# Turning blocks by DMA instead of TensorE in a recurrent-memory attention kernel

## The chip, the cores and the metric

The kernel runs on one core of one Trainium2 chip. The metric is the time of one execution on the device in microseconds (us), taken as the median of several runs.

## The reference, cut to what matters

```python
h  = x + A(_layernorm(x))                 # x: 2048 tokens x 512
h2 = h + B(_layernorm(h))                 # B: layernorm, 512 -> 1792, gelu, 1792 -> 512

def A(x):                                 # 64 segments of 32 tokens, one after the other
    mem = mem0                            # 8 rows
    for s in range(64):
        h = concat([mem, x[32*s : 32*s+32]])            # 40 rows
        q, k, v = h @ Wq, h @ Wk, h @ Wv                # 32 heads of 128
        p = softmax(where(mask, q @ k.T * scale, -1e9))
        o = (p @ v) @ Wo
        mem = o[:8]                                     # goes into the next segment
        outs.append(o[8:])
    return concat(outs)
```

The memory rows are a recurrence: segment s+1 cannot start its projections before segment s has its output projection.

## The kernel before

All weights of part A lie in SBUF from the first 50 us on. Phase 1 handles the 64 segments in order; phase 2 is the MLP on four groups of 512 tokens. Four segments of 32 tokens make a *block* of 128 tokens (16 blocks, `bk`; `sg` is the segment within the block, 0 to 3).

The input rows of a block come by DMA into a slot of `xr`. `ln1(tb)` normalises block `tb` (statistics on VectorE, DVE, the root on GpSimd, POOL) into `xn`, and turns it: four 128x128 transposes on TensorE (PE) into PSUM (`quad`, line 619), then two copies into the stationary operands, `hT` (24 token columns of each segment, line 629) and `hB` (the last 8 token columns of each of the four segments, line 628). Their place in `hT` is taken by the 8 memory rows that the segment before leaves there (line 915).

A segment consists of parts, each a short list of PE instruction groups and of the work on other engines behind them:

- `Q0, Q1, K0, K1, V0, V1`: projections by halves of the heads, four groups each (`one_pass`, line 654). A group is four matmuls side by side in column strips (128*32), one for each quarter of the PSUM bank's partitions. Where two groups in a row use the same stationary operand, its load is left out (`keep`, `matmul_kept`, line 427); `BACK` names passes that run over the contraction in reverse to make that possible.
- A copy of the bank to `kqP` (ACT or DVE, lines 668 and 669) and a 32x32 DVE transpose (line 696) give K and Q by head; `ZC` (lines 666 and 722, POOL) collects query columns for the scores.
- `SC0, SC1`: scores of the rows that need the recurrence (line 796) on a prefilled mask (line 779), then the softmax: maximum `nmc` (804), exponential `EC` (808, ACT), `rsc` (811), `PC` (814), `PTC` (815).
- `PV0, PV1`: weighted sums (lines 826, 830), with row strips (32*128), into `quad`; copies to `OT` and `OTB`.
- `SA`: the scores of the other 24 rows (line 855) and their softmax `PA` (870, POOL or DVE), `PTA` (872). `PVA` (line 881, also 32*128) is their weighted sum, one segment later.
- `WO`: the output projection in eight units (line 909), a DVE transpose `TT` (921), and the additions into `hT` of the next segment and into `opT` (915).
- `F0, F1, FB`: projections of the `hB` rows of the next block (K, Q, V) and the output projection `wo_B` of the block before, which fill PE while the recurrence goes through other engines.
- `TR`: `ln1(bk + 3)` in `sg` 1, and `nat(bk - 2)` in `sg` 0.

`nat(bk)` turns a finished block of `opT` back to rows with four PE transposes into `quad` (line 946). `nat_add` adds them to `xr` on DVE (955), takes statistics for the second layernorm and stores the rows to `h_mid` (962). Both PSUM results of `TR` are read after PV1 of the same segment:

```python
elif name == "TR":
    if sg == 0 and bk > 1:
        after_pv1(nat(bk - 2))
    if s in (1, 2):
        after_pv1(ln1(s + 1))
    elif sg == 1 and bk + 3 < NTB:
        after_pv1(ln1(bk + 3))
```

The order on PE is written out in `ORDER`, one list for each `sg`: `("Q0", 0, 3)` is groups 0 to 2 of that part. `BANKS` gives each part a PSUM bank. The order on all other engines comes from a planner (`Sched.schedule`): every operation has an expected duration (`dur`), a time for handing over (`HOP`, 2.0 us after a DMA), a rank, and a bonus by kind (`BONUS`); it is put into the first gap of its engine that holds it. Where an operation has a choice of engine (`either`), the earliest end decides, with `LEAN` us added for DVE. A DMA is expected to take 0.07 us and a 390th of a us for each KB, plus the 2.0. Operations without a choice wait in the order so planned: an engine never passes over an instruction that waits. All DMAs are issued by one queue, SP's.

PE's instruction stream is cut into basic blocks ("lines") of about 256 instructions by `far` (line 318). Each ends with a conditional branch that is never taken; its target is the line after the next one, and a hint is marked at the start of each line except the first (`mark_branch_hint_location`).

Of the kernel before, what the change touches and what calls it, by code (L numbers as in the profile page):

```python
# [21 lines left out]
LINE_N, LINE_AT, LINE_HINT = 256, 192, 168  # L22
HALVES = ("kqP", "KA", "ZCm", "QA", "VS", "nmc", "EC", "rsc", "PC", "PTC", "OTm", "KB", "QTB", "VSB", "QT")
BONUS = {"EC0": 0.93, "EC1": -5.34, "KA0": 13.28, "KA1": -9.68, "KB0": 21.59, "KB1": 28.09, "OTB": 0.99, "OTm0": 1.34, "OTm1": 17.4,
         "OTx": 13.15, "PA": 5.1, "PC0": 10.61, "PC1": 1.08, "PTA": -17.15, "PTC1": 2.21, "QT0": 2.01, "QT1": 40, "QTB0": 40, "QTB1": -5.37,
         "SA": -0.92, "TT": 17.86, "TTB": 32.47, "VBD": -40, "VS0": 8.39, "VS1": -1.27, "VSB0": 3.04, "VSB1": 40, "ZCb": -29.51,
         "ZCm0": -8.01, "ZCm1": 4.83, "ag": -16.93, "ag2": 3.08, "hB": -4.35, "hTm": 40, "hTx": 40, "hd": 1.51, "hx": -40, "kqP0": -1.06,
         "kqP1": 22.77, "kqP2": -1.2, "kqP3": -8.45, "kqP4": -7.07, "kqP5": -5.84, "nma": 40, "nmc0": -3.19, "nmc1": 0.4, "opA": -6.6,
         "opB": 14.93, "ps": -5.46, "rs": -7.45, "rs2": 11.04, "rsa": 13.98, "rsc1": 1.67, "sma": 8.62, "st": -40, "st2": -14.59,
         "vd": 17.77, "xr": 40}  # L30
LEAN = 0.297
# [4 lines left out]
          (("Q0", 0, 1), ("K0", 0, 2), ("Q0", 1, 2), ("K0", 2, 3), ("Q0", 2, 4), ("K0", 3, 4), ("Q1", 0, 4), ("K1", 0, 4), ("SC0", 0, 1),  # L36
           ("V0", 0, 1), ("TR", 0, 1), ("PVA", 0, 1), ("V0", 1, 4), ("V1", 0, 1), ("SC1", 0, 1), ("F1", 0, 1), ("V1", 1, 2), ("PV0", 0, 1),
           ("V1", 2, 4), ("F0", 0, 2), ("WO", 0, 2), ("PV1", 0, 1), ("WO", 2, 8), ("F1", 1, 2), ("F0", 2, 4), ("F1", 2, 4), ("SA", 0, 1)),
          (("Q0", 0, 3), ("K0", 0, 2), ("Q0", 3, 4), ("K0", 2, 3), ("Q1", 0, 1), ("K0", 3, 4), ("K1", 0, 1), ("Q1", 1, 4), ("K1", 1, 4),
           ("SC0", 0, 1), ("V0", 0, 1), ("PVA", 0, 1), ("V0", 1, 4), ("V1", 0, 2), ("SC1", 0, 1), ("TR", 0, 1), ("PV0", 0, 1),  # L40
           ("F0", 0, 1), ("V1", 2, 4), ("WO", 0, 4), ("PV1", 0, 1), ("F0", 1, 3), ("WO", 4, 8), ("F0", 3, 4), ("F1", 0, 4), ("SA", 0, 1)),
          (("K0", 0, 3), ("Q0", 0, 1), ("K0", 3, 4), ("Q0", 1, 4), ("Q1", 0, 4), ("K1", 0, 4), ("SC0", 0, 1), ("V0", 0, 1), ("PVA", 0, 1),
           ("V0", 1, 2), ("TR", 0, 1), ("V0", 2, 3), ("V1", 0, 1), ("V0", 3, 4), ("V1", 1, 2), ("SC1", 0, 1), ("V1", 2, 4), ("PV0", 0, 1),
           ("F0", 0, 1), ("F1", 0, 2), ("F0", 1, 2), ("WO", 0, 2), ("PV1", 0, 1), ("WO", 2, 8), ("F1", 2, 3), ("F0", 2, 4), ("F1", 3, 4),
           ("SA", 0, 1)),
          (("Q0", 0, 3), ("K0", 0, 2), ("Q0", 3, 4), ("K0", 2, 4), ("Q1", 0, 4), ("K1", 0, 4), ("SC0", 0, 1), ("PVA", 0, 1), ("V0", 0, 2),
           ("FB", 0, 1), ("V0", 2, 4), ("V1", 0, 1), ("SC1", 0, 1), ("V1", 1, 2), ("FB", 1, 2), ("V1", 2, 3), ("PV0", 0, 1), ("V1", 3, 4),
           ("FB", 2, 3), ("TR", 0, 1), ("FB", 3, 4), ("WO", 0, 2), ("PV1", 0, 1), ("WO", 2, 8), ("FB", 4, 7), ("SA", 0, 1), ("FB", 7, 8)),
)
BANKS = (  # L50
    dict(Q0=4, Q1=7, K0=6, K1=5, V0=6, V1=7, SC0=4, SC1=4, F0=6, F1=5, FB=5, SA=7, WO=4),
    dict(Q0=4, Q1=7, K0=6, K1=5, V0=6, V1=7, SC0=4, SC1=4, F0=6, F1=5, FB=5, SA=7, WO=4),
    dict(Q0=4, Q1=7, K0=6, K1=5, V0=6, V1=7, SC0=4, SC1=4, F0=6, F1=5, FB=4, SA=7, WO=4),
    dict(Q0=4, Q1=7, K0=6, K1=5, V0=6, V1=7, SC0=4, SC1=4, F0=6, F1=7, FB=5, SA=7, WO=4),
)
BACK = (("Q1", "K1", "V0", "F1"), ("Q0", "Q1", "K0", "K1", "V0", "F1"), ("K0", "K1", "V0"), ("Q0", "K0", "K1", "V0"))
# [26 lines left out]
class Sched:  # L83
# [234 lines left out]
    def far(self, nc, e, zero):  # L318

        ops = self.streams["pe"]  # L320
        n, lines, cuts = 0, -1, []
        for i, o in enumerate(ops):
            line, at = divmod(n - LINE_AT, LINE_N)
            if line > lines and at >= LINE_HINT:
                assert at < 240
                cuts.append(i)
                lines = line
                n += 2
            n += o.ni + (len(o.waits) >= 2)
        home, mark, k = nc.cur_bb.parent, None, 0  # L330
        for i, o in enumerate(ops):
            if k < len(cuts) and cuts[k] == i:
                if k + 2 < len(cuts):
                    b = e.br_lt(zero, 0, on_true="line%d" % (k + 2), on_false="line%d" % k)
                    if mark is not None:
                        b.branch_hint(mark)
                    nc.switch_bb("line%d" % k, parent=home)
                    mark = e.mark_branch_hint_location()
                else:
                    e.br("line%d" % k)  # L340
                    nc.switch_bb("line%d" % k, parent=home)
                k += 1
            yield o
# [51 lines left out]
ALU = mybir.AluOpType  # L395
AX = mybir.AxisListType

P = 128
# [46 lines left out]
def build_kernel(nc, A_x, A_mem0, A_Wq, A_Wk, A_Wv, A_Wo, B_w1, B_b1, B_w2, B_b2, out):  # L445
# [3 lines left out]
    with st:  # L449
# [10 lines left out]
        hT = sb("hT", [P, RING, DC, SEG])  # L460
        hB = sb("hB", [P, RBLK, DC, SEG])
        xr = sb("xr", [P, XR, D])
# [142 lines left out]
        def ln1(tb):  # L605
# [8 lines left out]
                 reads=[("xr", tb % XR), ("ag", i), ("rs", i)], writes=[("xn", i)], dur=0.405)  # L614
            pb = qbf(128)
# [7 lines left out]
            def ev():  # L623
                src = pb.rearrange("p c (s t) -> p c s t", s=4)
                r0 = 4 * (tb % RBLK)
                dA = hT[:, r0:r0 + 4, :, 0:NA].rearrange("p s c t -> p c s t")
                dB = hB[:, tb % RBLK, :, :].rearrange("p c (s t) -> p c s t", s=4)
                S.either(copy2(dB, src[:, :, :, NA:SEG], 128), reads=QK, writes=[("hB", tb % RBLK)])
                S.either(copy2(dA, src[:, :, :, 0:NA], 384), reads=QK, writes=[("hTx", tb % RBLK)])
            return ev  # L630

        def mem0_T(bank):
            pb = psbf(bank)

            def tr(e):
                for cc in range(DC):
                    ins = e.transpose(pb[:, cc * MEM:(cc + 1) * MEM], m0[0:MEM, cc * P:(cc + 1) * P], ident[0:MEM, 0:MEM])
                return ins
            S.op("pe", tr, reads=["m0", "ident"], writes=[("ps", bank)], dur=0.2, mode=MF)
            S.op("act", lambda e: e.copy(hT[:, 0, :, NA:SEG], pb[:, 0:DC * MEM].rearrange("p (c m) -> p c m", c=DC)),  # L640
                 reads=[("ps", bank)], writes=[("hTm", 0)], dur=t_act(32))
# [36 lines left out]
        def pack_a(s):  # L678
            sl = s % RING
            return ("A", s), (lambda cc: hT[:, sl, cc, :]), [("hTx", (s // 4) % RBLK), ("hTm", sl)]  # L680
# [14 lines left out]
        def pair_T(dst, i, key):  # L695
            S.op("dve", lambda e: e.transpose(dst.bitcast(U32), kqP[:, i, :].bitcast(U32)), reads=[("kqP", i)], writes=[key], dur=0.445)  # L696
# [85 lines left out]
        def sc_mm(s, r, bank):  # L782
# [4 lines left out]
            def f(e):  # L787
                for i in range(4):
# [11 lines left out]
                 writes=[("ps", bank)], dur=0.116, mode=MC, ni=32)  # L800

        def sc_softmax(s, r, bank):
            v = ps[bank][:, 0:128].rearrange("p (a t) -> p a t", a=2)
            S.op("dve", lambda e: e.tensor_reduce(nmc[:, r, :], v, AX.X, ALU.max, negate=True), reads=[("ps", bank)], writes=[("nmc", r)], dur=0.287)  # L804
# [40 lines left out]
        def sa_mm(s, bank):  # L845
# [12 lines left out]
            S.op("pe", f, reads=[("QT", 0), ("QT", 1), ("KA", par, 0), ("KA", par, 1)], writes=[("ps", bank)], dur=0.24, mode=MC, ni=64)  # L858
# [9 lines left out]
            S.op("dve", lambda e: e.tensor_reduce(sma[:], SA[:], AX.X, ALU.add), ["SA"], ["sma"], dur=0.41)  # L868
# [48 lines left out]
        def wo(s, bank, mem=True, xrows=True):  # L917
# [4 lines left out]
            if mem:  # L922
                sl = (s + 1) % RING
                S.op("dve", lambda e: [halves_add(tt, q2, hT[64 * q2:64 * q2 + 64, sl, :, NA:SEG], slice(NA, SEG))(e) for q2 in range(2)][1],
                     reads=[("TT", par)], writes=[("hTm", sl)], dur=0.39)
# [6 lines left out]
        def wo_B(bk, bank):  # L932
# [5 lines left out]
                 reads=["TTB"], writes=[("opB", bk % 2)], dur=0.6)  # L938

        def nat(bk):  # L940
            pb = qbf(192)
            xs = xr[:, bk % XR, :]
# [8 lines left out]
        def nat_add(bk):  # L951
# [3 lines left out]
            S.op("dve", lambda e: e.tensor_tensor(x4, x4, pb, ALU.add), reads=QK + [("xr", bk % XR)], writes=[("xr", bk % XR)], dur=0.41)  # L955
            i = bk % 2
# [32 lines left out]
        hx0, xn0 = xr[:, 2:6, :], view(hT, 4 * DC * SEG, [P, TBS, D])  # L989
# [65 lines left out]
        for s in range(NS):  # L1055
# [29 lines left out]
            def part(name):  # L1085
# [26 lines left out]
                elif name == "TR":  # L1112
                    if sg == 0 and bk > 1:
                        after_pv1(nat(bk - 2))
                    if s in (1, 2):
                        after_pv1(ln1(s + 1))
                    elif sg == 1 and bk + 3 < NTB:
                        after_pv1(ln1(bk + 3))
# [153 lines left out]
```

## Time and profile before

| | |
|---|---|
| median of 8 runs | 861.92 us (859.62 to 865.55) |
| profiled execution, own time | 867.18 us |
| its span, first to last instruction | 865.5 us |
| PE matmuls, busy | 803.8 us, 22,285 instructions |
| DVE, ACT, POOL busy | 544.3, 587.1, 144.0 us |
| granted TensorE clock, mean | 0.984 |
| DMA moved | 40.45 MB, 47 GB/s mean |

The times of the runs spread over 6 us. The profiled execution is one of them in kind, and took 5.3 us more than the median. Times in the profile are those of that execution; busy times of PE include overlap of one matmul with the next, so a single duration (380 ns for a 128x512 matmul) is more than the distance at which they follow each other.

### The profile page before, as it was taken

Reading aid. Unit: us, or ns where it says so; the run is one execution under the profiler, and the core shown is the slowest. Engines: PE = TensorE matmul, PEld = TensorE weight load, DVE = VectorE, ACT = ScalarE, POOL = GpSimd, SP = SyncE. Lnnn points to the kernel's source line nnn. Section 1 sums busy time; section 2 is a strip of 40 time slices with the busy share of each in tenths; the row PEclk is TensorE's granted clock in tenths of the full one; section 3 lists DMA queues with packets and bytes.
Section 4 is the critical chain, followed back from the end, with each engine's and each line's share of the span. In section 5 each row is a group of like instructions: output and inputs, shape, how many; then the busy total and the mean of one; then the engine's idle time right before and its main releaser. Section 6 shows DMA issues by size and latency. Waiting matters only on the chain.

```text
span 865.5 us, 48049 instructions
## 1 busy us (share of the span) xinstructions
PE 803.8 (93%) x22285; PEld 438.1 (51%) x21141; DVE 544.3 (63%) x1683; ACT 587.1 (68%) x1602; POOL 144.0 (17%) x341
## 2 busy tenths in 40 slices
PE   2568899999999999899999999999999998889998
PEld 0134455555555555455555555555555554544443
DVE  2137676778777777677778786767676776532111
ACT  1237677878787878677878787878777776624442
POOL 3012111212121212111111111111111111042200
PEclk9879999999999999999999999999999999999999
DMA  8771001010101010101010101010101110601000
GB/s 337 278 226 40 3 5 28 16 29 16 32 14 34 12 34 10 28 15 29 16 28 17 27 17 28 11 27 11 28 11 29 34 28 9 219 16 48 25 25 25
DMA packets 35303, 40.45 MB, mean 47 GB/s; under 512 B 2452, under 2 KB 31004, under 8 KB 35100
## 3 DMA queue, kind: packets, MB, share of 16 engines
q1 hardware_dynamic: 35100, 37.38, 13.3%
q8 instruction: 172, 2.82, 1.3%
q14 instruction: 31, 0.25, 0.1%
HBM read 28.98 MB, written 8.39 MB: 43 GB/s over the span
## 4 chain that ended last, share of the span: by engine, by line
PE 84%; DVE 7%; DMA 3%; ACT 2%; issue 2%; SPq 1%; POOL 0%; DVEq 0%
PE ps L654 39%; PE ps L909 17%; PE ps L427 6%; PE quad L1169 6%; PE ps L1162 6%; PE quad L826 3%; PE ps L796 2%; PE quad L881 2%; PE ps L855 2%; DMA WQ<-in_A_Wq_dram 1%; DVE opT L937 1%; DMA xr<-in_A_x_dram 1%; ACT EC L808 1%; DVE QT L696 1%; SPq L757 1%
## 5 line engine op out<-in xcount | busy, mean ns | idle before, releaser
L909 PE MATMUL ps<-WO,OT 128*32 128x256 bf16 x4224 | 141.6, 276 | 7.0 <-issue 5.0
L654 PE MATMUL ps<-WV,hT 128*32 128x512 bf16 x1796 | 147.1, 387 | 0.2
L654 PE MATMUL ps<-WQ,hT 128*32 128x512 bf16 x1804 | 133.2, 384 | 3.9 <-DVE hT L915 3.9
L654 PE MATMUL ps<-WK,hT 128*32 128x512 bf16 x1736 | 127.8, 379 | 1.5 <-DVE hT L915 1.1
L909 PEld LDWEIGHTS ps<-WO,OT 128*32 128x32 bf16 x4224 | 102.8, 97 | 38.5 <-ACT OT L668 12.9
L669 ACT ACTIVATE kqP<-ps 128x512 bf16<-128x512 f32 x159 | 95.2, 599 | 30.6 <-PE ps L654 28.4
L668 ACT CAST OT<-quad 128x128 bf16<-128x128 f32 (+1 forms) x177 | 80.9, 457 | 35.6 <-PE quad L830 21.2
L668 ACT CAST kqP<-ps 128x512 bf16<-128x512 f32 x160 | 91.9, 583 | 16.0 <-PE ps L654 13.7
L870 POOL TENSOR_TENSOR PA<-SA,rsa 128x256 bf16<-128x256 f32 x64 | 40.9, 639 | 367.3 <-DVE rsa L869 342.3
L808 ACT ACTIVATE EC<-ps,nmc 128x64 f32<-128x64 f32 x256 | 78.0, 310 | 17.6 <-DVE nmc L804 13.0
L921 DVE STREAM_TRANSPOSE TT<-ps 128x256 f32<-128x256 f32 x66 | 29.7, 450 | 84.0 <-PE ps L909 84.0
L1165 ACT ACTIVATE WQ<-ps,b1t 128x512 bf16<-128x512 f32 x56 | 38.5, 687 | 61.5 <-PE ps L1162 61.0
L654 PEld LDWEIGHTS ps<-WQ,hT 128*32 128x32 bf16 x1804 | 48.7, 97 | 62.0 <-issue 25.2
L668 ACT CAST VS<-ps 128x512 bf16<-128x512 f32 x112 | 65.5, 585 | 20.6 <-PE ps L654 11.3
L654 PEld LDWEIGHTS ps<-WK,hT 128*32 128x32 bf16 x1736 | 47.7, 97 | 54.2 <-issue 16.5
L696 DVE STREAM_TRANSPOSE KALL<-kqP 128x256 uint32<-128x256 uint32 x160 | 64.9, 412 | 11.3 <-ACT kqP L668 11.0
L867 ACT ACTIVATE SA<-SA 128x256 f32<-128x256 f32 x64 | 26.7, 417 | 53.2 <-DVE SA L866 53.2
L696 DVE STREAM_TRANSPOSE QT<-kqP 128x256 uint32<-128x256 uint32 x128 | 55.1, 431 | 4.7 <-ACT kqP L669 4.2
L796 PEld LDWEIGHTS ps<-KALL,ZC 128*32 128x32 bf16 x2048 | 30.9, 96 | 49.7 <-DVE rsc L811 20.4
L1169 PE MATMUL quad<-WK,WQ 128*128 128x512 bf16 x224 | 54.4, 379 | 0.5 <-DVE xr L955 0.5
L654 PEld LDWEIGHTS ps<-WV,hT 128*32 128x32 bf16 x1796 | 40.9, 97 | 24.5 <-issue 13.5
L1213 DVE TENSOR_TENSOR WV<-quad,WV 128x512 bf16<-128x512 f32 x16 | 11.1, 691 | 66.0 <-PE quad L1169 66.0
(116 smaller groups left out, 1371.3 us busy)
## 6 DMA issues: line engine op xcount, KB each, us to landing
WV<-in_A_Wv_dram SPq DMA_DIRECT2D x4, 1024.0 KB, 6.5
WK<-in_A_Wk_dram SPq DMA_DIRECT2D x4, 1024.0 KB, 8.0
v_last<-VSB SPq DMA_DIRECT2D x64, 64.0 KB, 2.1
WQ<-in_A_Wq_dram SPq DMA_DIRECT2D x4, 1024.0 KB, 7.8
VBD<-v_last SPq DMA_DIRECT2D x64, 64.0 KB
WO<-in_A_Wo_dram SPq DMA_DIRECT2D x4, 1024.0 KB, 9.3
WK<-in_B_w_dram SPq DMA_DIRECT2D x2, 1792.0 KB, 13.3
xr<-in_A_x_dram SPq DMA_DIRECT2D x16, 128.0 KB, 2.2
```

The costliest lines, as they stand in the source:

```text
L427: return e.add_instruction(mybir.InstMatmult(name="I-%d" % (4000000 + _kept[0]), engine=mybir.EngineType.PE, start_tensor_calc=start, stop ...
L654: ins = e.matmul(o, l, m, start=start, stop=stop, tile_position=(0, 32 * j), skip_group_check=True)
L668: return {"act": (lambda e: e.copy(out, src), t_act(n, ps_)), "dve": (lambda e: e.tensor_copy(out, src), 0.165 + 1.0e-3 * n * fast)}
L669: return {"act": (lambda e: e.mul(out, src, scale_), t_act(n, ps_)), "dve": (lambda e: e.tensor_scalar(out, src, scale_, None, ALU.mult), ...
L696: S.op("dve", lambda e: e.transpose(dst.bitcast(U32), kqP[:, i, :].bitcast(U32)), reads=[("kqP", i)], writes=[key], dur=0.445)
L796: ins = e.matmul(ps[bank][32 * j:32 * j + 32, 64 * sl:64 * sl + 64], ZC[:, par, h, :], rhs, start=False, stop=(i == 3), tile_position=(0, ...
L808: ins = e.activation(EC[:, r, sl, :], ps[bank][:, 64 * sl:64 * sl + 64], ACTF.Exp, bias=nmc[:, r, sl:sl + 1], accum_out=smc[:, r, sl:sl + 1])
L870: pa = lambda e: e.tensor_tensor(PA[:], SA[:], bc(rsa), ALU.mult)
L909: ins = e.matmul(ps[bank][32 * j:32 * j + 32, 0:256], lhs(slot(h)), wo_cols(h, b), start=(k == 0), stop=(k == 15), tile_position=(0, 32 * ...
L1162: ins = e.matmul(ps[bank][:, 0:SBT], W1[:, cc, fc * P:(fc + 1) * P], hnT_of(k, cc // 2)[:, cc % 2, :], start=(cc == 0), stop=(cc == DC - 1))
L1165: S.op("act", lambda e: e.activation(gT[:, fc, :], ps[bank][:, 0:SBT], ACTF.Gelu_apprx_tanh, bias=b1t[:, fc:fc + 1], scale=1.0), reads=[(" ...
L1169: S.op("pe", lambda e: e.matmul(quad[:, t, :], gT[:, fc, t * P:(t + 1) * P], W2[:, fc, :], start=(fc == 0), stop=(fc == FC - 1)), reads=[" ...
```

## The change

From token block 2 on, `ln1` no longer uses PE: a DMA transpose on SP's queue writes the whole turned block into `hT`, whose layout is changed so that the four segments of a block lie side by side, and POOL copies the last eight columns of each segment from there to `hB`. `nat` for blocks 0 to 13 turns `opT` by a DMA transpose into a new tile `xT`, and the addition to `xr` reads `xT` on DVE or POOL. Blocks 0 and 1 at the start and 14 and 15 at the end stay on PE. `TR` no longer defers anything until after PV1. The first line of PE's stream gets a hint mark too, at instruction 128 of the first line (`LINE_FIRST`), and its branch moves from 168 to 200. `ORDER`, `BANKS`, `BACK`, `BONUS` and `LEAN` are new, and some expected durations are altered. The new order places PVA beside PV0 (`sg` 0 and 1) or PV1 (`sg` 3).

```diff
-LINE_N, LINE_AT, LINE_HINT = 256, 192, 168
+LINE_N, LINE_AT, LINE_HINT, LINE_FIRST = 256, 192, 168, 128
...
-LEAN = 0.297
+LEAN = 10.341
...
 ORDER = (
-          (("Q0", 0, 1), ("K0", 0, 2), ("Q0", 1, 2), ("K0", 2, 3), ("Q0", 2, 4), ("K0", 3, 4), ("Q1", 0, 4), ("K1", 0, 4), ("SC0", 0, 1),
-           ("V0", 0, 1), ("TR", 0, 1), ("PVA", 0, 1), ("V0", 1, 4), ("V1", 0, 1), ("SC1", 0, 1), ("F1", 0, 1), ("V1", 1, 2), ("PV0", 0, 1),
-           ("V1", 2, 4), ("F0", 0, 2), ("WO", 0, 2), ("PV1", 0, 1), ("WO", 2, 8), ("F1", 1, 2), ("F0", 2, 4), ("F1", 2, 4), ("SA", 0, 1)),
+          (("Q0", 0, 3), ("TR", 0, 1), ("Q0", 3, 4), ("K0", 0, 4), ("Q1", 0, 4), ("K1", 0, 4), ("SC0", 0, 1), ("V0", 0, 4), ("V1", 0, 2),
+           ("SC1", 0, 1), ("V1", 2, 4), ("F0", 0, 1), ("PVA", 0, 1), ("PV0", 0, 1), ("F0", 1, 3), ("WO", 0, 3), ("PV1", 0, 1),
+           ("F0", 3, 4), ("WO", 3, 8), ("F1", 0, 1), ("SA", 0, 1), ("F1", 1, 4)),
...
+          (("Q0", 0, 3), ("TR", 0, 1), ("Q0", 3, 4), ("K0", 0, 4), ("Q1", 0, 4), ("K1", 0, 4), ("SC0", 0, 1), ("V0", 0, 4), ("V1", 0, 1),
+           ("PVA", 0, 1), ("SC1", 0, 1), ("F0", 0, 1), ("V1", 1, 4), ("PV0", 0, 1), ("F0", 1, 2), ("SA", 0, 1), ("WO", 0, 2),
+           ("PV1", 0, 1), ("WO", 2, 8), ("F0", 2, 4), ("F1", 0, 4)),
...
-            if line > lines and at >= LINE_HINT:
+            if early is None and line == 0 and at >= LINE_FIRST:
+                early = i
+                n += 1
+            if line > lines and at >= (LINE_HINT if line else 200):
...
+            if i == early:
+                mark = e.mark_branch_hint_location()
...
-        hT = sb("hT", [P, RING, DC, SEG])
+        hT = sb("hT", [P, DC, RING, SEG])
...
+        xT = sb("xT", [P, D])
...
+            r0 = 4 * (tb % RBLK)
+            if tb > 1:
+                S.dma(lambda e: e.dma_start_transpose(hT[:, :, r0:r0 + 4, :].rearrange("p c s t -> p c (s t)"), xn[:, i, :]), 128, reads=[("xn", i)],
+                      writes=[("hTx", tb % RBLK)] + [("hTm", r0 + k) for k in range(4)])
+                dB = hB[:, tb % RBLK, :, :].rearrange("p c (s t) -> p c s t", s=4)
+                S.op("pool", lambda e: e.tensor_copy(dB, hT[:, :, r0:r0 + 4, NA:SEG]), reads=[("hTm", r0 + k) for k in range(4)], writes=[("hB", tb % RBLK)], dur=0.3)
+                return None
...
         def nat(bk):
+            if bk < NTB - 2:
+                S.dma(lambda e: e.dma_start_transpose(xT[:].rearrange("p (c d) -> p c d", c=DC), opT[:, bk % 2].rearrange("p c t -> p (c t)")), 128,
+                      reads=[("opA", bk % 2, k) for k in range(4)] + [("opB", bk % 2)], writes=["xT"])
+                xo = xr[:, bk % XR, :]
+                add = lambda e: e.tensor_tensor(xo, xo, xT[:], ALU.add)
+                S.either({"dve": (add, 0.45), "pool": (add, 1.15)}, reads=["xT", ("xr", bk % XR)], writes=[("xr", bk % XR)])
+                nat_stats(bk)
+                return None
...
                 elif name == "TR":
                     if sg == 0 and bk > 1:
-                        after_pv1(nat(bk - 2))
+                        nat(bk - 2)
                     if s in (1, 2):
-                        after_pv1(ln1(s + 1))
+                        ln1(s + 1)
                     elif sg == 1 and bk + 3 < NTB:
-                        after_pv1(ln1(bk + 3))
+                        ln1(bk + 3)
```

## The prediction

> **What bounds the kernel now.** I read the page's totals first, then a table of stretches, then who TensorE (PE) waited for, then PE's timeline of one block of four segments.
>
> ```profile
> PE 803.8 (93%) x22285; PEld 438.1 (51%) x21141; DVE 544.3 (63%) x1683; ACT 587.1 (68%) x1602; POOL 144.0 (17%) x341
> ```
>
> ```profile
> 299.90:342.50 42.60, 42.37 (x1364) 23.80 (x1276) 32.49 (x104) 33.49 (x96) 7.49 (x18) 1.00 0.08 23
> ...
> 323.66:370.48 46.82, 44.03 (x1360) 24.41 (x1280) 32.49 (x103) 33.53 (x97) 7.49 (x18) 0.96 0.08 23
> ```
>
> The second fence has two stretches of one block (start and end, length; busy time of PE, weight loads, DVE, ACT, POOL; clock; DMA share; GB/s). An ordinary block takes 42.60 us and PE works in 42.37 of it, at full clock: some fifteen such blocks are nearly three quarters of the span, and there PE is the limit. So a PE instruction removed shortens the kernel, as long as no other chain takes over. The other block lasts 4.2 us longer; the waits say why.
>
> ```profile
> PE ps L909 <- issue: 5.0, 2, 2.6
> PE ps L654 <- DVE hT L915: 5.0, 6, 1.1
> PE quad L826 <- issue: 3.3, 1, 3.3
> ...
> PE ps L796 <- DVE KALL L696: 2.1, 9, 0.2
> ```
>
> Columns: total us, times, longest. Three waits are "issue", with no releaser: 3.29 us at 54.27 in the first segment, 2.55 at 363.88 and 2.49 at 761.07. After the first two the clock is halved for some microseconds, which makes the second one cost 4.2 us. The wait for L915 (memory rows of the next segment) occurs only where filler work is missing, at both ends. One block on PE:
>
> ```profile
> 317.19 0.40 PE L654 MATMUL ps<-WV,hT 128*32 128x512 bf16 x4
> 317.52 0.40 PE L946 MATMUL quad<-ident,opT 128*128 128x128 bf16 x4
> 317.85 0.37 PE L881 MATMUL quad<-PTA,VS 32*128 32x24 bf16 x32
> 318.15 0.83 PE L654 MATMUL ps<-WV,hT 128*32 128x512 bf16 x12
> ```
>
> The first column is the start. Four matmuls of the 128*32 shape normally take 0.216 us, yet the next group starts 0.33 us later: 0.11 us goes on the change of tile shape. The four transposes (128*128) then hold PE for 0.33 us.
>
> **What the skill says.** "TensorEngine Tiling (Array Packing)", Key Properties: changing the tiling mode drains TensorE. The trace agrees, with 0.11 us on entry. "Runtime: NRT & Kernel Launch", Instruction fetch mechanics: instructions arrive in 16 KiB blocks of 256, and a branch outside the window costs a fetch. The trace has 172 packets of 16 KiB on the instruction queue; the first stall comes after 344 matmul and 345 weight-load records, about 704 of the planner's instructions (192 + 2 x 256), so at a block boundary. "VectorE: DVE Perf Modes", The three transpose paths: 1309 ns for a 128x128 transpose by DMA. No run yet shows one. "DMA: Bandwidth & Descriptors", Rules for kernel authors: a transpose next to ordinary DMAs needs nothing; all transposes here are on SP's queue.
>
> **The change, part by part.**
>
> Transposes. ln1 for token blocks 2 to 15 and nat for 0 to 13 leave PE: 28 groups of four. Each held PE 0.33 us (317.52 to 317.85; the ln1 group at 329.84 to 330.17 likewise), with one shape change in it: 28 x 0.33 = **9.2 us**.
>
> Shape changes from the new order. Before, PVA stood alone in every segment. Now it stands next to PV0 or PV1, which have the same 32*128 shape, in three of the four segments. That drops one way in and one way out, 48 times. The way in is 0.11 us; the way out is not separable in the trace, so 0 to 0.11. That is 5.3 to 10.6 us, and I take **7.9**.
>
> The hint. Line k+2 is announced from line k; line 0 had no mark, so the first conditional branch announced nothing. The stall at 54.27 is at the boundary that this branch should have announced, and the new mark sits about 70 instructions ahead of it. Gone with the stall goes the half clock that follows it: the 32 matmuls of the value pass ran from 57.98 to 61.34, 3.4 us instead of 1.7, and WO 2.42 instead of 1.93. So 3.3 us at least, 5.5 at most; PV1's DVE result comes just before, so nothing is late in its place. I take **4.5**. If the mark misses: 0.
>
> PSUM copies. Two ACT copies of ln1 (262 and 478 ns) go from each block; nat's addition of 421 ns on DVE now reads SBUF and has POOL as an alternative at 1.15 us. ACT is at 33.49 of 42.60 us, so its relief brings nothing itself. LEAN of 10.3 us makes the planner shun DVE for copies that have a choice: the 16 VS copies (691 ns) and 15 OT copies (291 ns) that DVE has now may go to ACT, 15.4 us over 16 blocks, about 1 us each. Against the 0.74 saved that leaves ACT near 34 of 41.5 us, 82%, still covered by PE.
>
> SP's queue. 28 transposes join, two a block. In the stretch around 300 to 345 us SP issues four stores and four loads of VBD, one h_mid store and one x load. nat's transpose must precede the overwriting of opT two segments (some 20 us) on, and ln1's result is needed a block later at the earliest. Cost taken: 0, hidden by that distance; without it, a transpose's landing time each.
>
> POOL. Two instructions a block now wait for a landing: the hB copy (planned at 0.3 us) and, most likely, nat's addition. The planner puts a landing at 0.07 + 128/390 + 2.0 = 2.4 us. The nearest rows:
>
> ```profile
> xr<-in_A_x_dram SPq DMA_DIRECT2D x16, 128.0 KB, 2.2
> h_mid<-xr SPq DMA_DIRECT2D x16, 128.0 KB, 2.1
> ```
>
> (us to landing last), and on POOL's timeline
>
> ```profile
> 316.67 0.29 POOL L666 COPY ZC<-QT 128x128 bf16<-128x128 bf16 x1 [0.67 <-DVE QT L696]
> 318.13 0.29 POOL L666 COPY ZC<-QT 128x128 bf16<-128x128 bf16 x1 [1.17 <-DVE QT L696]
> ```
>
> Plain copies of this size land in 2.1 to 2.2 us; four of the skill's 128x128 prices in a row are 5.2, an estimate. I take 3.0: POOL's instruction is 0.6 us late. Queued behind it on POOL are the ZC copies, for which PE's SC waits, and PA. They have 0.67 to 1.5 us of idle time before them, so 0.6 costs nothing; 5.2 would cost (next part).
>
> Tighter waits from the new order. From SC to its PV, the softmax (nmc 290, two EC with reads, rsc 165, PC 292, PTC 312 ns) needs about 2.15 us; by the durations above the new order leaves 2.15 to 2.5. From K1 to SC1 it leaves in segment kind 0 0.12 + 0.86 + 0.43 = 1.41 us, where a copy of 583, a DVE transpose of 412 ns and three handovers (some 0.3) need 1.3; before, 1.83. After WO it keeps 1.1 us or more of filler, and L915's rows took 1.15 us from WO's end at 713.23 to the pass at 714.38. So places that had slack are at the edge: 0 to 0.25 us a segment, I take 0.07 x 60 = **+4**.
>
> Sum. The profiled execution took 867.18 us (span 865.5 and 1.7 around it), 5.3 over the median of 861.92; 4.2 of that is the stall at 363.88, which I take as this execution's own. 867.18 - 4.2 = 863.0; less 9.2, 7.9 and 4.5 is 841.4; plus 4 is 845.4. Against the median, 844.3. I say 845.
>
> **The rivals.**
>
> The chain takes over (chance 0.16). Each segment's memory rows come out of WO of the one before. Where block 15 has almost no filler, a segment still took 10.49 us (714.38 to 724.87, 0.54 of it other transposes), against 10.65 with filler. If the chain lets a segment fall only to 10.5, the blocks gain 0.6 x 15 = 9 us, and with the hint the time is 848; if it lets nothing fall, the hint's 4.5 alone gives 857. For it: the 1.41 us above. Against: the waits for KALL, 0.2 at most, show hardly any chain waiting now, and PE was busy 99% in the block. Missing hint or a new fetch stall (2.5 to 4.2 us each) lies in this range too.
>
> POOL stands waiting for transposes (0.17, slower). If a transpose lands in 5.2 us, POOL is 2.8 us late, the ZC copy behind it eats about 1.2 of idle time, and 1.6 us reach SC and the memory chain: 28 x 1.6 = 45, so 890. It decides when the exposed part passes 21 / 28 = 0.75 us each, a landing of about 4.3 us. For it: the skill's 1309 ns, that POOL takes its instructions in the order written, and that the planner uses a plain copy's duration. Against it: POOL is busy only 17%; 1024 KB of WV land in 6.5 us and 128 KB in 2.2, so some 1.6 us of a landing do not grow with size and the four parts need not add up; and some of the waits will fall where POOL has 3 to 7 us of idle time, as before PA.
>
> Transposes do not pay, because they are issued late or delay instruction pages: 2.5 to 4.2 us per late page, two or three pages, 850 to 857. Chance 0.05.
>
> **How the numbers follow.** The forecast (836 to 851) has 0.62. Its low end takes both shape ends and the whole stall: 861.9 - 5.5 - 9.2 - 10.6 = 836.6; the stall at 761.07 gone as well makes 834. The high end of 864 takes in the chain rival whole and the first microseconds of the POOL rival. Left out is most of the latter, 0.15, and little below. A change of 0.2%, 1.7 us, is about what a measurement can tell. Faster 0.80: the forecast, the chain, the late pages, less their worst ends. Slower 0.18: POOL and the worst of the others. Same 0.02.
>
> **What would show it.** Right: a block near 41.4 us with PE busy over 98%, no 128*128 groups inside blocks 2 to 13, no "issue" wait near 54 us, landings under 4 us for xT and hT. Wrong: POOL's ZC or xr lines waiting for DMA and PE's L796 waiting for ZC; PE waiting at L654 for L915 inside the blocks; a landing above 4.3 us; the stall still at the same place.

## The result, and the profile after

The changed kernel takes 854.74 us (median of 19 runs, 849.06 to 865.5), the kernel before 862.41 us in the runs beside it. The ratio is 0.9909, 95% interval 0.989 to 0.9928. It is faster, by 7.7 us and not by the 17 that were forecast. Its runs lie further apart than those of before; late instruction pages (pieces of PE's instruction stream that do not arrive in time, explained below) are the likely reason for that, and they hold most of the missing microseconds. The profiled execution took 858.69 us (span 856.8). Every ratio here compares only those runs that lie within 1.5% of the fastest of their kernel, so where a kernel's runs lie far apart its ratio comes from the better ones and can be lower than the medians beside it suggest.

The profile's totals of the kernel after:

```profile
PE 791.9 (92%) x22173; PEld 432.9 (51%) x21613; DVE 519.8 (61%) x1637; ACT 583.8 (68%) x1578; POOL 170.3 (20%) x397
```

PE has 12 us less work, POOL 26 us more. Stretches of one block each of the kernel after (columns as before: length; busy time of PE, weight loads, DVE, ACT, POOL; clock; DMA share; GB/s):

```profile
310.00:351.77 41.77, 41.65 (x1348) 23.76 (x1305) 30.79 (x100) 33.18 (x94) 9.42 (x22) 1.00 0.15 31
...
220.00:268.15 48.15, 44.60 (x1368) 25.33 (x1328) 31.46 (x101) 33.75 (x96) 9.35 (x22) 0.93 0.13 26
```

An ordinary block is 41.8 us instead of 42.9 (from one SA to the SA four segments on, the median of the blocks without a long stall), and PE is busy in all but 0.1 of it. But two blocks are some 6 us longer, at a clock of 0.93. Who PE waited for, in the kernel after (us, times, longest):

```profile
PE quad L836 <- issue: 8.0, 3, 4.1
...
PE ps L806 <- POOL ZC L676: 5.6, 3, 4.4
PE ps L664 <- DVE hT L925: 4.9, 6, 1.1
PE ps L664 <- issue: 3.4, 1, 3.4
PE ps L1183 <- issue: 3.1, 1, 3.1
```

Before, "issue" stood for three waits (3.29, 2.55 and 2.49 us). Now there are four of 3 us and more: at 54.15 in the first segment, at 234.03 and 490.40 inside blocks, at 749.70 near the end. So the first stall, which the hint was to remove, is still at its place in this execution. And there is a wait that before did not have: SC at 74.44 for the ZC copy on POOL, 4.37 us. POOL's timeline there, in the kernel after:

```profile
67.82 0.22 POOL L615 TENSOR_SCALAR rst<-agg 128x1 f32<-128x1 f32 x1
73.78 0.29 POOL L624 COPY hB<-hT 128x128 bf16<-128x128 bf16 x1 [5.74 <-DMA hT<-xn]
74.01 0.29 POOL L676 COPY ZC<-QT 128x128 bf16<-128x128 bf16 x1
```

The hB copy stood 5.74 us for the landing of a transpose, and ZC right behind it. The new rows of the DMA list (us from issue to landing last), and PE where PVA now stands beside PV0:

```profile
hT<-xn SPq DMA_TRANSPOSE x14, 4.5
xT<-opT SPq DMA_TRANSPOSE x14, 3.7
```

```profile
333.06 0.41 PE L664 MATMUL ps<-WV,hT 128*32 128x512 bf16 x4
333.40 0.37 PE L891 MATMUL quad<-PTA,VS 32*128 32x24 bf16 x32
333.62 0.30 PE L836 MATMUL quad<-PTC,VS 32*128 32x16 bf16 x16
```

PVA holds PE for 0.22 us here, against the 0.30 in the prediction's timeline (317.85 to 318.15), where a group of another shape followed it: at these two places the way out of a shape costs 0.08 us. The way in is 0.12 (333.06 to 333.40, less 0.216).

Why does PE stand for 3 us with no releaser? The trace has 173 packets of 16,384 bytes on the instruction queue. PE's stream arrives in such pieces, called pages here; PE's 43,786 matmul and weight-load records would make 171 pages at 256 a page. They usually follow each other by 3.86 us (median). Around the stall at 234.03 they start at 218.48, 223.79, 230.84 and 235.05: one is missing between the second and the third, and the last starts 1.0 us after PE has stopped. At 490.40 it is the same (475.10, 480.26, 487.94, 491.38). So a page did not come ahead of time, and was fetched when PE had run out. That is the reading of these two stalls; the packets do not name the engine that they are for. In the same window SP did this, in the kernel after:

```profile
222.07 2.26 SPq L767 DMA_DIRECT2D VBD<-v_last  x4
224.43 1.24 SPq L621 DMA_TRANSPOSE hT<-xn  x1
235.04 1.34 SPq L952 DMA_TRANSPOSE xT<-opT  x1
```

ln1's transpose is issued right behind the four VBD loads; its packets of 256 bytes fly from 225.7 to 228.6, in the gap. Both kinds of transposes move 128 KB, but those into hT fly 2 to 3 us and those into xT mostly 0.8.

### The profile page after: what moved, and what is told of

It is laid out like the page before. It is cut to its first block, busy times and chain, and to the rows that moved or that the text cites. A ratio compares the mean times of both kernels' runs of the same rounds, so it can differ in the third digit from the quotient of the medians.

```text
span 856.8 us, 48411 instructions
## 1 busy us (share of the span) xinstructions
PE 791.9 (92%) x22173; PEld 432.9 (51%) x21613; DVE 519.8 (61%) x1637; ACT 583.8 (68%) x1578; POOL 170.3 (20%) x397
## 4 chain that ended last, share of the span: by engine, by line
PE 85%; ACT 5%; DMA 3%; DVE 3%; issue 3%; SPq 1%; POOL 0%; DVEq 0%
PE ps L664 42%; PE ps L919 18%; PE ps L1183 6%; PE quad L1190 6%; PE ps L430 3%; PE quad L836 3%; PE ps L806 2%; PE quad L891 2%; PE ps L865 2%; ACT EC L818 1%; ACT kqP L679 1%; DMA WQ<-in_A_Wq_dram 1%; ACT kqP L678 1%; DMA xr<-in_A_x_dram 1%; PE quad L840 1%
## 5 line engine op out<-in xcount | busy, mean ns | idle before, releaser
L919 PE MATMUL ps<-WO,OT 128*32 128x256 bf16 x4224 | 145.5, 280 | 1.2 <-ACT OT L678 0.8
L664 PE MATMUL ps<-WQ,hT 128*32 128x512 bf16 x1920 | 130.8, 383 | 5.1 <-DVE hT L925 4.9
L664 PE MATMUL ps<-WV,hT 128*32 128x512 bf16 x1984 | 132.6, 382 | 0.0
L678 ACT CAST OT<-quad 128x128 bf16<-128x128 f32 (+1 forms) x192 | 85.0, 443 | 55.6 <-PE quad L840 50.0
L664 PE MATMUL ps<-WK,hT 128*32 128x512 bf16 x1736 | 119.1, 379 | 0.0
L919 PEld LDWEIGHTS ps<-WO,OT 128*32 128x32 bf16 x4224 | 100.3, 98 | 29.8 <-ACT OT L678 8.9
L678 ACT CAST kqP<-ps 128x512 bf16<-128x512 f32 x160 | 93.6, 585 | 16.1 <-PE ps L664 14.7
L706 DVE STREAM_TRANSPOSE KALL<-kqP 128x256 uint32<-128x256 uint32 x160 | 69.3, 433 | 52.0 <-ACT kqP L678 51.6
L676 POOL COPY ZC<-QT 128x128 bf16<-128x128 bf16 x128 | 38.3, 299 | 239.7 <-DVE QT L706 239.6
L664 PEld LDWEIGHTS ps<-WQ,hT 128*32 128x32 bf16 x1920 | 47.3, 97 | 71.4 <-issue 19.3
L664 PEld LDWEIGHTS ps<-WK,hT 128*32 128x32 bf16 x1736 | 48.2, 96 | 63.2 <-issue 26.4
L678 ACT CAST VS<-ps 128x512 bf16<-128x512 f32 x128 | 75.1, 587 | 2.2 <-PE ps L664 1.5
L664 PEld LDWEIGHTS ps<-WV,hT 128*32 128x32 bf16 x1984 | 47.8, 96 | 30.6 <-ACT kqP L678 7.2
```

The costliest lines, as they stand in the source:

```text
L664: ins = e.matmul(o, l, m, start=start, stop=stop, tile_position=(0, 32 * j), skip_group_check=True)
L676: "pool": (lambda e: e.tensor_copy(out, src), 0.16 + 1.05e-3 * n)}
L678: return {"act": (lambda e: e.copy(out, src), t_act(n, ps_)), "dve": (lambda e: e.tensor_copy(out, src), 0.165 + 1.0e-3 * n * fast)}
L919: ins = e.matmul(ps[bank][32 * j:32 * j + 32, 0:256], lhs(slot(h)), wo_cols(h, b), start=(k == 0), stop=(k == 15), tile_position=(0, 32 * ...
```

## The experiments

Ratios are to the kernel before, in runs on the same chip; its medians lay between 862.8 and 866.0 us. "Block" is the median length of a block without a long stall in the profile, "late pages" are issue waits of over 1 us between 100 and 700 us. The before kernel's profile has one of these, the changed one's two. Each kernel has one profile, so a count of late pages is that of one execution.

**The parts by themselves.** Hint alone, on the kernel before:

```diff
-            if line > lines and at >= LINE_HINT:
+            if early is None and line == 0 and at >= LINE_FIRST:
+                early = i
+                n += 1
+            if line > lines and at >= (LINE_HINT if line else 200):
```

> The kernel before with the hint mark in the first line and its branch moved from 168 to 200, nothing else. If the hint does what the prediction took (removes the stall near 54 us and its half clock), 861.9 - 4.5, about 857.5, and no issue wait near 54 us. If the hint does nothing, as the profile after suggests (a stall of 4.10 us at 54.15 still there), 862 within 1 us and the stall in its place.

857.77 us, ratio 0.9944 (0.9919 to 0.997): 4.8 us, close to the 4.5 of the prediction. The profiled execution still had a stall of 3.76 us at its place and took 865.3 us; 13 of 22 runs lay between 853.9 and 857.8, the others reached up to 866.5. So it seems that the hint works in some executions and not in others. The kept profiles agree: of the nine kernels here that have the hint, three show no stall near 54 us, and six show one of 3.4 to 4.2 us; all eight without it show one.

Transposes alone, on the order of before:

```diff
+            if tb > 1:
+                S.dma(lambda e: e.dma_start_transpose(hT[...], xn[:, i, :]), ...)
...
+            if bk < NTB - 2:
+                S.dma(lambda e: e.dma_start_transpose(xT[...], opT[...]), ...)
```

> The kernel before with the 28 groups of transposes moved to DMA and the hT layout that goes with it; the PE order, banks, bonuses and the hint of before. If a group is worth 0.33 us of PE time as the prediction took, a clean block is 0.66 us shorter (42.9 to about 42.2) and the time is 9 us lower, 853. If POOL's wait for a landing reaches PE in the blocks, the clean block stays at 42.9 or grows. If transposes make late instruction pages, the profile shows more issue waits than before (3) and the time is near 860.

880.05 us, ratio 1.0203 (1.0159 to 1.0247), 17 us slower. Who PE waited for, in its longest execution (889.81 us):

```profile
PE quad L833 <- issue: 13.7, 4, 3.9
PE ps L916 <- issue: 9.9, 4, 3.1
PE ps L803 <- issue: 4.7, 7, 1.5
```

Blocks without a stall are about 42.4 us, 0.5 less (0.66 was forecast). But seven pages are late, six of them 5 to 13 us after a transpose into hT was issued. POOL's waits do not reach PE inside the blocks.

New order with all transposes on PE: `if tb > 1` and `if bk < NTB - 2` of the changed kernel become `if False`, TR goes just before PVA, and its results are read after PV1 again. The hint, the banks and the bonuses stay those of the changed kernel.

> The changed kernel with all transposes back on PE (TR just before PVA, its results read after PV1), the new order, banks, bonuses and hint kept. If the saved shape changes are worth 7.9 us and the hint nothing, a clean block is 42.9 - 0.5 = 42.4 us and the time 854 to 858. If the page stalls come with the new order and not with the transposes, the profile shows 4 issue waits or so and the time is 858 to 864. If they come with the transposes, 3 at most.

868.52 us, ratio 1.0077 (1.0051 to 1.0103). No late page, but nearly every block had a wait of 1.1 to 1.3 us of TR or PVA for the copies out of quad (ACT, L678), and was 44.2 us. The new order is made for a quad without transposes. Less its wait a block is 42.9 us, no shorter than before, so this run does not show the saving by fewer shape changes.

**The start.** Token blocks 2 and 3 back on PE (`if tb > 1` becomes `if tb > 3`). As these have PSUM results again, TR also moves to just before PVA in all four lists, and the results are read after PV1:

> The changed kernel with the two transposes of the start (token blocks 2 and 3) back on PE, TR noted before PVA. If the wait of SC for ZC behind the hB copy (4.37 us at 74.4 in the profile after, with the half clock that follows) costs what it seems, 4 to 7 us less than the changed kernel, 848 to 851, and no such wait. If something else holds that segment, the time stays at 854.7.

853.71 us, ratio 0.9762 (0.9705 to 0.9819). The ratio rests on the two shortest of nine runs (838.70 and 844.99); the median of all nine is 0.9885 of that of before, hardly less than the changed kernel's, so by the median the 848 to 851 did not come. In the profile the wait for ZC was gone, and from the first SA to the fifth it took 46.8 us instead of the changed kernel's 52.0. Late pages remained: three, of 3.1 to 3.8 us.

**What about the transposes loses the pages?** First the layout. hT as `[P, RBLK, DC, 4, SEG]`, so that a transpose writes 1,024 bytes in a row in each partition; on the old order, on the changed kernel, and on it with the start repaired:

```diff
-        hT = sb("hT", [P, DC, RING, SEG])
+        hT = sb("hT", [P, RBLK, DC, 4, SEG])
```

> The run with the transposes alone on the order of before (880 us), with hT laid out so that the 512 columns a block's transpose writes in a partition lie together, as xT's do. Theory: instruction pages that PE should have had ahead of time are lost while a transpose is in flight; the hT transposes fly 2.3 to 3.7 us, the xT ones 0.8 to 1.4, and the stalls come about 10 us after an hT flight. If the scattered destination makes the flights long, they fall to about 1 us, most of the 8 issue waits of the blocks go, and the time is 853 to 858. If the flight is long for another reason (the source, the slot), nothing changes and it stays at 880. If late pages come from the changed PE stream and not from transposes, it stays at 880 with short flights.

> The changed kernel with that same block-wise hT. On the theory of flights, flights of about 1 us, none or one issue wait inside the blocks instead of two, and 848 to 851. If flights don't set the stalls, 854.7 as the changed kernel.

> The changed kernel with block-wise hT and the two transposes of the start back on PE. If both repairs add up, 5 us at the start and 3 to 6 us of page stalls below the changed kernel: 843 to 847, the fastest so far. If they don't, about 850.

877.22 us (1.0134, 1.007 to 1.0199), 860.25 (0.9866, 0.9786 to 0.9947; three of six runs) and 855.22 (0.9809, 0.9736 to 0.9882; four of six runs), with flights behind the loads of 1.8 to 3.1 us and five, three and four late pages. Neither the short flights nor the lower times came. The layout is not the cause; as the flights did not become shorter, these runs say nothing on whether long flights lose pages.

Then the traffic. On the old order with both transfers, ln1's as a plain copy, which leaves the rows unturned:

```diff
-                S.dma(lambda e: e.dma_start_transpose(hT[...], xn[:, i, :]), ...)
+                S.dma(lambda e: e.dma_start(hT[...], xn[:, i, :].rearrange("p (c t) -> p c t", c=DC)), ...)
```

> The run with the transposes alone on the order of before, where each of the 14 transposes into hT is a plain copy of the same 128 KB by DMA to the same columns (256 bytes a piece), so the rows of blocks 2 to 15 are not turned. If it is turning that loses the pages, the stalls after these transfers go and the time is 853 to 858. If any DMA of this size and piece does it, it stays near 880.

858.76 us, ratio 0.9921 (0.9892 to 0.995). The copies stand in the same place and fly nearly as long (2.0 to 2.8 us), PE's stream is the same, and one page was late instead of seven:

```profile
PE quad L833 <- issue: 5.6, 2, 3.3
...
PE ps L916 <- issue: 1.4, 1, 1.4
```

So it is the turning, and neither the traffic nor the length of its flight alone. The medians say the same: 858.76 us, against 877.22 on the same chip for the run with the block-wise hT.

Then one kind of transpose at a time; nat's alone and ln1's alone on the old order, nat's alone in the changed kernel. The kind that goes back to PE is read after PV1 again, and in the changed kernel TR moves to just before PVA:

```diff
-            if tb > 1:
+            if False:
```

> The kernel before with nat's 14 transposes alone on DMA; ln1 on PE. Theory: the pages are lost to the ln1 transposes, which fly some 3 us, not to nat's of 0.8 us. Then no more issue waits in the blocks than before (0 or 1), clean blocks of 42.6, and before - 4.6, a ratio of 0.995. If any transpose loses pages, some four issue waits and a time equal to before or above.

> The kernel before with ln1's 14 transposes alone on DMA; nat on PE. On the same theory nearly all of the loss of the run with both: six or more issue waits in blocks 2 to 12, and about 14 us more than before (1.016). If nat's transposes lose the pages, or only both together, before - 4.6 (0.995).

> The changed kernel (new order, hint) with ln1 back on PE for all blocks, TR just before PVA, nat on DMA. On the theory: clean blocks of 41.8 + 0.33 = 42.1, no start wait, 0 or 1 issue wait in the blocks, 848 to 851 and runs that differ less. If TR makes PE wait for quad as in the run with both on PE (1.3 us a block), 865.

nat alone: 856.38 us, ratio 0.9917 (0.9881 to 0.9953), blocks of 42.5, no late page. ln1 alone: 865.96 us, ratio 1.0027 (1.0003 to 1.0052), blocks of 42.8; its profile caught the shortest run (861.46 us) with one late page of 1.2 us, while the runs reach 880. That is far less of a loss than the 14 us that were expected, though these transposes stand behind the VBD loads and fly as long (1.9 to 2.9 us): the two kinds together cost more than the sum, and most of the loss comes only with both. Why is open. One thing that differs is where PE's pages end, as the groups on PE are others. nat alone in the changed kernel: **840.34 us**, ratio 0.9719 (0.9675 to 0.9764), six runs between 835.5 and 842.1, blocks of 42.2. That is 8 us better than expected; its profile has no stall near 54 us either. Its waits:

```profile
PE ps L919 <- issue: 1.2, 1, 1.2
PE ps L1183 <- issue: 0.5, 3, 0.2
```

The changed kernel without its hint:

> The changed kernel without the hint in the first line. If the hint is worth in it what the run with the hint alone showed (5 to 6 us in most executions), 858 to 860 where the changed kernel has 854.7, a ratio of 0.996 to before. If the lines cut elsewhere shift the late pages as well, the difference can be of either sign by 3 to 6 us.

857.44 us, ratio 0.9852 (0.9795 to 0.9909; three of six runs). Its interval and that of the changed kernel overlap; with four late pages in the profile and runs from 848 to 863, it says nothing on the hint.

Last the place. ln1's transpose waits for the h_mid store that follows nat's, in the changed kernel, on the old order, and in the changed kernel with the start repaired:

```diff
+            stored[0] = S.dma(lambda e: e.dma_start(hd[:, bk, :], xs), ...)
...
-                      writes=[...])
+                      writes=[...], after=[stored[0]])
```

> The changed kernel where ln1's transpose is made to wait for the landing of the h_mid store that follows nat's transpose, so that SP issues it some 6 us after xT's and not right behind the four VBD loads. If the VBD loads make the hT flights long (2.1 to 3.1 us) and the long flights lose the pages, flights of about 1 us, no late page in the blocks, and 845 to 849, with only the wait at the start left. If ln1's turning loses pages wherever it stands, two or three issue waits and 854 to 860 as the changed kernel.

> The same wait in the run with both transposes on the order of before (880 us, ratio 1.020). If the place behind the VBD loads is the cause, clean blocks of 42.3 and a ratio near 0.99, as with nat's transposes alone less 0.33 us a block. If ln1's turning loses pages wherever it stands, 1.01 to 1.02.

> The changed kernel with that wait and with token blocks 2 and 3 on PE. If both repairs work, clean blocks of 41.8 and no start wait: 838 to 842, a ratio of 0.970, level with or a little below the run with ln1 on PE throughout (840.3, 0.972). If ln1's turning loses pages wherever it stands, 850 to 855.

**840.6 us** (0.9723, 0.9688 to 0.9758), 859.03 (0.9951, 0.9922 to 0.998) and **833.04** (0.9651, 0.9616 to 0.9686). What PE waited for in the first of them, which differs from the changed kernel by this edit alone (the profile is of its longest execution, 848.78 us):

```profile
PE ps L808 <- POOL ZC L678: 5.6, 3, 3.8
...
PE ps L1185 <- issue: 4.3, 4, 3.8
PE quad L838 <- issue: 3.7, 2, 3.4
```

The waits for ZC are as before the edit, and the issue waits stand near 54 us and in phase 2; inside the blocks there is none of over 1 us. SP in the last of the three:

```profile
223.58 1.24 SPq L954 DMA_TRANSPOSE xT<-opT  x1
227.29 0.35 SPq L985 DMA_DIRECT2D h_mid<-xr  x1
229.78 1.21 SPq L623 DMA_TRANSPOSE hT<-xn  x1
```

and all that PE waited for "issue", and for ZC, in its whole span of 829.2 us:

```profile
PE ps L808 <- POOL ZC L678: 1.8, 2, 1.3
...
PE ps L1185 <- issue: 0.5, 3, 0.2
...
PE quad L838 <- issue: 0.2, 1, 0.2
```

Away from the VBD loads the hT transposes fly 0.8 us, as xT's mostly do, and land in 2.6 us. In the changed kernel there is no late page left between 100 and 700 us; with the start repaired too, no stall of 3 us anywhere, and six runs between 829.2 and 836.4. This version beats both kernels, by 3.5% against the one before.

On the old order all of the 17 us lost are won back, and 4 more. Its profile, the longest of its executions, still has two late pages, at 408.8 and 539.0 us. The last hT transposes before them were issued 36 and 34 us earlier, so these two cannot be laid to them; the kernel before, too, has one late page without any DMA transpose.

The wait moves the transpose away from the loads, but in the same step from some 10 us ahead of the next xT transpose to 6 us behind one and 36 ahead of the next, and to another point of PE's stream. Which of these counts, no run tells apart.

The four profiles by stretches, in us (the stretches begin and end at an SA; the blocks are segments 4 to 60):

| | before | changed | changed, apart | apart, start repaired |
|---|---|---|---|---|
| to the first SA | 57.7 | 58.4 | 57.7 | 53.9 |
| first four segments | 52.0 | 52.0 | 52.6 | 45.7 |
| fourteen blocks | 603.5 | 598.1 | 585.9 | 584.9 |
| last three segments | 36.0 | 31.8 | 32.1 | 31.8 |
| the rest | 116.3 | 116.5 | 118.6 | 112.9 |
| span | 865.5 | 856.8 | 846.9 | 829.2 |

## Why the prediction was wrong

**SP's queue: the step that failed.** Its cost was taken as 0, hidden by the distance to where the data is needed. In the blocks the data was indeed in time, but PE's instruction pages were not. With the 28 transposes in the place that the change gives them, the fourteen blocks took 598.1 us; with ln1's issued apart, nothing else altered, 585.9, so 12 us in these executions, and 14 us between the medians (854.74 and 840.6). With this loss gone the same kernel lies within the forecast of 836 to 851. The prediction had it as a rival ("two or three pages, 850 to 857") and gave it 0.05; the time, and the two late pages inside the blocks, are those of this rival.

What is shown: turning is needed (the plain copy in the same place lost one page, not seven), and the place is needed. The explanation is not complete. Most of the loss came only with both kinds of transposes on the queue, and whether the loads, the distance to the other transposes or the point of PE's stream makes the place a bad one is open. How the page gets lost, whether its announcement is dropped or its packets wait, no run shows.

**Hint: the size fits, the mechanism only in part.** By itself it gave 4.8 us where 4.5 were forecast. But the stall was to be gone, and the sign of being wrong, "the stall still at the same place", came: 4.10 us at 54.15 in the changed kernel's profile, and a stall in six of nine profiles with the hint. That the median came out at 4.8 is in part luck: it depends on in how many executions the hint takes effect.

**Transposes off PE: nearly right.** 0.66 us a block was forecast. Blocks fell by 0.5 on the old order with both kinds on DMA (42.9 to 42.4), by 0.4 with nat's alone and by 0.1 with ln1's alone, so the two groups were not each worth 0.33.

**Shape changes and tighter waits: net size nearly right.** 7.9 us less 4 us of tighter waits, 3.9 net, was the forecast. The new order, with its banks and bonuses, made blocks 0.3 to 0.6 us shorter at equal transposes (42.5 to 42.2 with nat's alone, 42.4 to 41.8 with both), 4 to 8 us in all. How much of that the shape changes give is not shown. The tighter waits, for which +4 stood in the sum, hardly came: PE is busy in 41.65 of 41.77 us. Together the blocks gained 1.1 x 14 = 15 us, where the sum had 13.

**POOL: the mechanism was right, once, and the threshold wrong.** The prediction let POOL's waits decide from a landing of 4.3 us, with 1.2 us of idle time as cover. ln1's landings were 4.5 us, and POOL stood 77.6 us for them in all, but in the blocks SC did not wait for it. At the start, where three transposes and four VBD loads came together and the planner had put ZC behind an hB copy, it cost one wait of 4.37 us and a half clock after it; with that repaired the first four segments took 5.2 us less (46.8 against 52.0). The landing taken, 3.0 us, was 0.7 to 1.5 too low, and the other estimate, 5.2, too high.

**Both ends: no term of their own.** The first four segments lost by POOL what the new order saved there, so that they took 52.0 us in both kernels. The last three fell from 36.0 to 31.8. With everything repaired the kernel takes 833.0, 11 us less than the 844.3 of the sum against the median. So that 840.6 falls near the forecast is also luck: losses left in it offset gains that the sum did not have.

**The chain of memory rows** as the new bound did not come: the waits of L664 for L925 are six and 4.9 us, at both ends only, as before.

## What to carry to other kernels

A DMA that lands in time can still cost: here instruction pages of the engine that sets the time came late, and the profile shows that only as waits with no releaser, beside a wider spread of the runs. When work is moved to a queue, look at what stands beside it there, and try another place before giving it up: the same 28 transposes gave 855 us with most of ln1's right behind four loads, and 841 us with ln1's issued elsewhere. And before an in-order engine is given an instruction that waits for a landing, look at what the planner puts behind it in the places where the pattern is not yet regular.

## What the runs showed of the hardware

- A DMA transpose of 128x512 bf16 within SBUF held SP for 1.2 us in most cases and landed after 2.4 to 4.1 us (xT, changed kernel). Its packets flew mostly 0.8 us in places apart, and 2 to 3 us right behind four loads of 64 KB.
- A page that comes late stopped PE for 1.2 to 4.7 us, and after most of these stalls the granted clock was halved for 3.4 or 6.8 us. The longer ones made a block 4 to 6 us longer.
- A plain copy of the same size in the same place lost one page where the transposes lost seven; with ln1's transposes alone in that place one page was late too.
- In the places shown, going into another tile shape cost PE 0.11 to 0.12 us, coming back 0.08.
